# Four accumulator banks in the first expert layer, branch hints one body ahead, and a written order on three engines

## The chip, the core and the metric

The kernel runs on one core of a Trainium2 chip. The metric is the device time of one execution in microseconds (us). The core has a matrix engine (PE, with a separate weight-load side, PEld), a vector engine (DVE), a scalar engine (ACT), a general engine (POOL) and a sync engine (SP). Each has its own instruction stream and waits for the others by semaphores. An engine's sequencer also runs branches and register loads; those are not counted as busy time. Code is brought to the engines by DMA, in its own two queues ("instruction" in the profile's table of queues), beside the data.

## What is computed

Two stages run one after the other. The first is a recurrent attention over 4 batches, 8 heads, 768 steps and a head width of 64; the kernel does it in chunks of 128 steps. The second is a mixture of 8 experts, each a two-layer network, with one expert per token and no token dropped:

```python
logits = x @ w_gate                      # x: 3072 tokens x 512
expert_idx = np.argmax(logits, axis=1)
gate_w = probs[np.arange(N), expert_idx]
for e in range(E):                       # 8 experts
    h = np.maximum(x_sorted[lo:hi] @ w1[e], 0.0)   # 512 -> 1024
    y_sorted[lo:hi] = h @ w2[e]                    # 1024 -> 512
return gate_w[:, None] * y
```

How many tokens an expert has is known only at run time.

## The kernel before

**Attention and routing.** A loop over 24 steps (6 chunks of 4 batches) does the attention. After each chunk, `logits` and `place` find each token's expert and its place in that expert's list. The logits of a chunk stand in the one accumulator bank of the tag "lg" (line 299), and DVE reads them there at lines 319 and 320. The last chunk's routing is woven on PE with the first 256 tokens of expert 0 ("early": `xTa`, `hTa`, `oa`). Then `cnt` (lines 433 and 434), also in the bank "lg", counts the tokens of every expert. DVE turns the counts into `arm`, eight small integers (lines 437 to 445).

**The eight jobs.** One job per expert (loop at line 469). A job has a body for each possible width, from 128 to 512 columns (tokens) in steps of 32: 13 bodies, 5 for expert 0. `tc.Switch` (line 479) makes ACT and PE branch to the body that `arm` asks for; in the last job POOL branches too. A body is: the first layer, eight fills of one accumulator bank each (`layer1`, f = 0 to 7: four accumulating products, which the profile counts as 8 MATMUL), each emptied by ACT with Relu into `hT`; then `turn`, 16 transposes of the next job's tokens, copied out by ACT; then the second layer, one tile of 128 tokens at a time (`layer2`), copied out by ACT into `o`. Each body begins with a hint that names its own exit (printed as line 479) and ends with a branch to the code behind all bodies (printed as the last lines, 590). There the next job's branch stands. So each boundary between jobs has two branches per engine: out of the old body, and into the new one.

**Accumulator banks.** There are eight: "tr" has 3, "sc" 2, "y" 2 and "lg" 1. `layer1` takes the two of "sc" in turn, so PE can fill f = 0 and 1 and must then wait until ACT has emptied f = 0.

**Order.** Inside the bodies PE and ACT follow the written order (line 478). Around them a scheduler places the work: it put all eight loads of `arm` into registers ahead of the first branch, and it spread POOL's indirect gathers (`xs` from `x_d`) and scatters (`o` to the output) over the jobs, so that a job's last two scatters run a job later. SP brings `w1t` and `w2t` (2 MB each) for the job after next as soon as a buffer comes free. Behind the eight jobs a branch skips code for experts with more than 512 tokens, which these inputs don't need.

Of the kernel before, what the change touches and what calls it, by code (L numbers as in the profile page):

```python
# [12 lines left out]
F32 = mybir.dt.float32  # L13
# [7 lines left out]
P = 128  # L21
# [29 lines left out]
def kernel(  # L51
# [11 lines left out]
    nc = tc.nc  # L63
    B, H, S, D = q.shape
    N, DM = out.shape
    E = w_gate.shape[1]
# [4 lines left out]
    DT = DM // P  # L71
    FT = F // P
    W = 512
    TC = W // P
    EARLY = 256
# [9 lines left out]
    def ps(tag, bufs, name):  # L85
        return psum.tile([P, 512], F32, tag=tag, name=name, bufs=bufs)
# [25 lines left out]
    def rt(shape, name, dt=F32):  # L112
        return route.tile(shape, dt, tag=name, name=name)
# [23 lines left out]
    def weights(pool, e):  # L137
        w1t = pool.tile([P, 1, DT, F], F32, tag="w1t", name="w1t")
        w2t = pool.tile([P, 1, FT, DM], F32, tag="w2t", name="w2t")
        nc.sync.dma_start(w1t, w1v[:, ds(e, 1), :, :])  # L140
        nc.sync.dma_start(w2t, w2v[:, ds(e, 1), :, :])
        return w1t, w2t

    first = ctx.enter_context(tc.tile_pool(name="first", bufs=1))
    xs2 = [first.tile([P, TC, DM], F32, tag=f"xs{i}", name=f"xs{i}") for i in range(2)]
# [3 lines left out]
    def gather(xs, idx, tiles, rows=N):  # L149
        for t in tiles:  # L150
            nc.gpsimd.indirect_dma_start(  # L151
                out=xs[:, t, :], out_offset=None, in_=x_d[0:rows, :],
                in_offset=bass.IndirectOffsetOnAxis(ap=idx[:, t : t + 1], axis=0), bounds_check=rows - 1,
                oob_is_err=False)
# [22 lines left out]
    def turn(xs, xT, tiles, evict):  # L177
        for t in tiles:
            tr = ps("tr", 3, "trs").rearrange("p (a t) -> p a t", a=DT)
            for dt in range(DT):  # L180
                nc.tensor.transpose(tr[:, dt, :], xs[:, t, ts(dt, P)], ident)
            evict(out=xT[:, :, ts(t, P)], in_=tr)

    def layer1(n, xT, w1t, hT, f):
        hp = ps("sc", 2, "hp")[:, 0:n]
        for dt in range(DT):
            nc.tensor.matmul(hp, lhsT=w1t[:, 0, dt, ts(f, P)], rhs=xT[:, dt, 0:n], start=(dt == 0),  # L187
                             stop=(dt == DT - 1))
        nc.scalar.activation(out=hT[:, f, 0:n], in_=hp, func=AF.Relu)  # L189

    def layer2(n, hT, w2t, o, t):

        m = min(n - t * P, P)
        parts = P // m if m in (P // 4, P // 2) else 1
        y = ps("y", 2, "ye")
        c = DM // parts
        for f in range(FT):
            for j in range(parts):
                nc.tensor.matmul(y[j * m : j * m + m, 0:c], lhsT=hT[:, f, t * P : t * P + m],  # L199
                                 rhs=w2t[:, 0, f, ts(j, c)], start=(f == 0), stop=(f == FT - 1))  # L200
        for j in range(parts):
            nc.scalar.copy(out=o[0:m, t, ts(j, c)], in_=y[j * m : j * m + m, 0:c])  # L202

    def scatter(o, idx, tiles):
        for t in tiles:
            done = nc.gpsimd.indirect_dma_start(  # L206
                out=out[:, :], out_offset=bass.IndirectOffsetOnAxis(ap=idx[:, t : t + 1], axis=0), in_=o[:, t, :],
                in_offset=None, bounds_check=N - 1, oob_is_err=False)

            tc.declare_no_dep(done.ins, group="scatters", reason="other rows of the output")  # L210
            tc.add_to_no_dep_group("scatters", done.ins)


    with ExitStack() as actx:
# [191 lines left out]
        for n in range(len(steps)):  # L406
# [6 lines left out]
            last, done = done, retain(n)  # L413
# [6 lines left out]
        with tc.manual_schedule(engines={mybir.EngineType.PE}):  # L420
            turn(xs2[0], xTa, range(EARLY // P), nc.vector.tensor_copy)
            for f in range(FT):
                layer1(EARLY, xTa, wa[0], hTa, f)
                if f != 4:
                    next(rest, None)
            for _ in rest:
                pass
            for t in range(EARLY // P):
                layer2(EARLY, hTa, wa[1], oa, t)
# [6 lines left out]
    arm = rt([P, E], "arm", I32)  # L436
    nc.vector.tensor_copy(ne, cnt)

    STEP, LEAST, MOST = 32, P // 32, W // 32
# [8 lines left out]
    PE, ACT, POOL = mybir.EngineType.PE, mybir.EngineType.Activation, mybir.EngineType.Pool  # L448


    mp = ctx.enter_context(tc.tile_pool(name="mp", bufs=2))
    keep2 = ctx.enter_context(tc.tile_pool(name="keep2", bufs=1))
    o2 = [keep2.tile([P, TC, DM], F32, tag=f"o{i}", name=f"o{i}") for i in range(2)]
    for t in o2:
        nc.vector.memset(t, 0.0)
    sets = [wa, weights(keep2, 1)]
    cols = [(src_i[:, ts(e, TC)], dst_i[:, ts(e, TC)]) for e in range(E)]
    HALF = EARLY // P

    gather(xs2[1], cols[0][0], range(HALF, TC))  # L460
    gather(xs2[0], cols[1][0], range(TC))
    xT = mp.tile([P, DT, W], F32, tag="xTs", name="xTs")
    turn(xs2[1], xT, range(HALF, TC), nc.vector.tensor_copy)

    def regs(e, engines):
        return {g: nc.engines[g].value_load(arm[0:1, e : e + 1], min_val=0,
                                            max_val=MOST - LEAST - (EARLY // STEP if e == 0 else 0)) for g in engines}

    for e in range(E):
        w1t, w2t = sets[e]  # L470
        skip = EARLY if e == 0 else 0
        arms = MOST - LEAST + 1 - skip // STEP
        engines = [PE, ACT] + ([POOL] if e == E - 1 else [])
        which = regs(e, engines)
        if e + 1 < E:
            xTn = mp.tile([P, DT, W], F32, tag="xTs", name="xTs")
        hT = mp.tile([P, FT, W], F32, tag="hT", name="hT", bufs=1)
        with tc.manual_schedule(engines={PE, ACT}):
            for a in tc.Switch(which, arms):
                n = STEP * (LEAST + a)  # L480
                for f in range(FT):
                    layer1(n, xT[:, :, skip:], w1t, hT, f)
                if e + 1 < E:
                    turn(xs2[e % 2], xTn, range(TC), nc.scalar.copy)
                tiles = -(-n // P)
                for t in [tiles - 1] + list(range(tiles - 1)):
                    layer2(n, hT, w2t, o2[e % 2], t)
                    if e == E - 1:
                        scatter(o2[e % 2], cols[e][1], [t])
        if e + 1 < E:  # L490
            tiles = range(TC - HALF) if e == 0 else range(TC)
            scatter(o2[e % 2], cols[e][1][:, HALF:] if e == 0 else cols[e][1], tiles)
            xT = xTn
        if e + 2 < E:
            gather(xs2[(e + 1) % 2], cols[e + 2][0], range(TC))
            sets.append(weights(first if e % 2 == 0 else keep2, e + 2))


    most = rt([P, 1], "most")
    over = rt([P, 1], "over", I32)  # L500
    nc.vector.tensor_reduce(most, ne, axis=AX.X, op=ALU.max)
    nc.vector.tensor_scalar(out=over, in0=most, scalar1=float(W), scalar2=None, op0=ALU.is_gt)
    more = nc.values_load(over[0:1, 0:1], min_val=0, max_val=1)
    with tc.If(more > 0), tc.tile_pool(name="op", bufs=1) as op:

# [51 lines left out]
        for j in range(OV):  # L557
            ev = nc.sync.value_load(whose[0:1, j : j + 1], min_val=0, max_val=E - 1)
            w1t, w2t = weights(keep2, ev)
            gather(xs2[j % 2], osrc_i[:, ts(j, TC)], range(TC))  # L560
            xT = mp.tile([P, DT, W], F32, tag="xTs", name="xTs")
            hT = mp.tile([P, FT, W], F32, tag="hT", name="hT", bufs=1)
            turn(xs2[j % 2], xT, range(TC), nc.vector.tensor_copy)
            for f in range(FT):
                layer1(W, xT, w1t, hT, f)
            for t in range(TC):
                layer2(W, hT, w2t, o2[j % 2], t)
            scatter(o2[j % 2], odst_i[:, ts(j, TC)], range(TC))
# [25 lines left out]
```

## Time and profile before

| | |
|---|---|
| time, median of 3 runs | 649.59 us (635.12 to 657.23) |
| profiled execution, its own time | 627.53 us |
| its span, first to last instruction | 625.7 us |
| PE busy | 563.8 us (90%) |
| ACT busy | 123.8 us (20%) |
| POOL busy | 118.8 us (19%) |
| DVE busy | 108.5 us (17%) |
| granted TensorE clock, mean | 0.947 |

The span falls into two parts: attention and routing up to about 227 us, then the eight jobs. Start times of the jobs' first layers on PE are 227.47, 245.54, 298.64, 352.27, 409.37, 457.84, 512.39 and 563.62 us; their widths in this run are 128, 416, 416, 448, 352, 416, 384 and 416 columns. In a row of a timeline the bracket gives the idle time just before the group, and what ended it; "issue" there means that the engine waited for nothing the profile shows, as it does while its sequencer stands at a branch.

### The profile page before, as it was taken

The page shows a single profiled execution, that of the slowest core. Times are in us where ns is not written, and L with a number is a line of the kernel's source. Part 1 is how long each engine was busy: PE and PEld are TensorE (multiplying, and loading weights), DVE is VectorE, ACT ScalarE, POOL GpSimd, SP SyncE. Part 2 cuts the span into 40 slices and gives each one's busy share as a digit, 9 for nine tenths or more (in the row PEclk, how much of TensorE's full clock was granted, in tenths as well). Part 3 has the DMA queues.
Part 4 walks back from the last instruction along what each step waited for, and adds up shares of the span by engine and source line. Part 5 has one row for each costly group of instructions (what it writes and reads, how often), then busy time and mean ns, then how long its engine had stood idle before and what let it go on. Part 6 is the DMA issues. An engine that isn't in the chain of part 4 may idle for free.

```text
span 625.7 us, 7784 instructions
## 1 busy us (share of the span) xinstructions
PE 563.8 (90%) x3160; PEld 371.6 (59%) x3160; DVE 108.5 (17%) x291; ACT 123.8 (20%) x245; POOL 118.8 (19%) x156
## 2 busy tenths in 40 slices
PE   4999999999999988799799989969979996999990
PEld 4988989898988664364355445436435543545540
DVE  2445555466453220000000000000000000000000
ACT  2223232323232211130012012002001201201100
POOL 8331312222220433002102200210310010000011
PEclk9997979899999999899899979999998997999996
DMA  9964647956120449513504410450550314000011
GB/s 186 211 126 124 137 129 213 316 124 159 34 89 14 132 125 381 192 47 137 186 0 170 134 75 18 170 187 0 190 183 0 139 43 147 0 4 20 4 37 50
DMA packets 96476, 72.50 MB, mean 116 GB/s; under 512 B 77946, under 2 KB 77946, under 8 KB 96384
## 3 DMA queue, kind: packets, MB, share of 16 engines
q1 hardware_dynamic: 88096, 52.46, 31.4%
q0 software_dynamic: 5120, 12.60, 5.9%
q10 hardware_dynamic: 3168, 6.29, 2.7%
q8 instruction: 48, 0.79, 0.6%
q14 instruction: 44, 0.36, 0.2%
HBM read 60.84 MB, written 14.68 MB: 121 GB/s over the span
## 4 chain that ended last, share of the span: by engine, by line
issue 56%; PE 28%; POOL 8%; DVE 4%; DMA 1%; POOLq 1%; SPq 0%; DVEq 0%
PE y L288 7%; POOL out_dram L206 4%; PE sc L260 4%; POOL xs L151 4%; PE tr L246 4%; PE y L284 4%; PE lg L308 3%; PE new L269 2%; PE hp L187 2%; PE trx L303 2%; DVE am L262 1%; DMA q<-in_q_dram 1%; DVE xT L305 0%; DVE state L276 0%; SPq L232 0%
## 5 line engine op out<-in xcount | busy, mean ns | idle before, releaser
L187 PE MATMUL hp<-xTs,w1t 128*128 128x416 f32 (+4 forms) x512 | 177.9, 509 | 31.5 <-ACT hT L189 27.8
L187 PEld LDWEIGHTS hp<-xTs,w1t 128*128 128x128 f32 x512 | 98.4, 204 | 111.4 <-issue 66.5
L199 PE MATMUL ye<-w2t,hT 128*128 128x512 f32 (+3 forms) x640 | 164.0, 455 | 0.0
L199 PEld LDWEIGHTS ye<-w2t,hT 128*128 128x128 f32 (+3 forms) x640 | 74.8, 155 | 84.2 <-issue 83.2
L206 POOL DMA_INDIRECT out_dram<-o,dst x30 | 29.8, 995 | 294.3 <-ACT o L202 236.7
L189 ACT ACTIVATE hT<-hp 128x416 f32<-128x416 f32 (+4 forms) x64 | 30.0, 480 | 178.5 <-PE hp L187 123.7
L288 PE MATMUL y<-vs,am 128*128 128x64 f32 x384 | 59.8, 276 | 1.6 <-DVE am L262 0.9
L288 PEld LDWEIGHTS y<-vs,am 128*128 128x128 f32 x384 | 54.5, 202 | 4.5 <-issue 1.8
L202 ACT COPY o<-ye 128x512 f32<-128x512 f32 (+3 forms) x40 | 17.7, 444 | 144.6 <-PE ye L199 144.3
L151 POOL DMA_INDIRECT xs<-x_d,src x30 | 30.3, 1009 | 72.6 <-PE ye L199 35.5
L262 DVE TENSOR_TENSOR am<-sc,causal 128x512 f32<-128x512 f32 x48 | 31.3, 685 | 41.7 <-PE sc L260 41.7
L284 PE MATMUL y<-stb,qT 128*128 128x128 f32 x160 | 37.6, 319 | 0.0
L260 PE MATMUL sc<-qT,kT 64*128 64x128 f32 x384 | 36.3, 300 | 0.9 <-DVE am L262 0.9
L279 POOL COPY stb<-state 64x256 f32<-64x256 f32 x40 | 19.6, 490 | 80.0 <-DVE state L276 78.9
L241 POOL TENSOR_TENSOR vs<-v,dec 128x512 f32<-128x512 f32 x24 | 25.4, 1062 | 38.5 <-PE new L269 25.7
L260 PEld LDWEIGHTS sc<-qT,kT 64*128 64x128 f32 x384 | 28.9, 196 | 5.2 <-issue 4.2
L291 ACT COPY xg<-y 128x512 f32<-128x512 f32 x24 | 14.1, 589 | 84.4 <-PE y L288 84.4
L284 PEld LDWEIGHTS y<-stb,qT 128*128 128x128 f32 x160 | 25.6, 202 | 1.3
L246 PE MATMUL tr<-ident,qs 128*128 128x128 f32 x96 | 18.5, 318 | 7.0 <-DVE qs L240 7.0
L308 PE MATMUL lg<-wg,xT 128*128 128x8 f32 x192 | 24.5, 254 | 0.3
L308 PEld LDWEIGHTS lg<-wg,xT 128*128 128x128 f32 x192 | 23.4, 192 | 1.7 <-DVE xT L305 1.2
L248 ACT COPY qT<-tr 128x512 f32<-128x512 f32 x24 | 14.1, 587 | 37.6 <-PE tr L246 37.6
(111 smaller groups left out, 340.4 us busy)
## 6 DMA issues: line engine op xcount, KB each, us to landing
w1t<-in_moe_w_dram SPq DMA_DIRECT2D x8, 2048.0 KB, 8.0
w2t<-in_moe_w_dram SPq DMA_DIRECT2D x8, 2048.0 KB, 12.0
q<-in_q_dram SPq DMA_DIRECT2D x24, 256.0 KB, 4.6
k<-in_k_dram SPq DMA_DIRECT2D x24, 256.0 KB, 3.2
v<-in_v_dram SPq DMA_DIRECT2D x24, 256.0 KB, 4.4
x_d<-xg ACTq DMA_DIRECT2D x6, 1024.0 KB, 4.4
xs<-x_d,src POOLq DMA_INDIRECT x30, 3.5
out_dram<-o,dst POOLq DMA_INDIRECT x30, 7.1
```

The costliest lines, as they stand in the source:

```text
L151: nc.gpsimd.indirect_dma_start(out=xs[:, t, :], out_offset=None, in_=x_d[0:rows, :], in_offset=bass.IndirectOffsetOnAxis(ap=idx[:, t : t + ...
L187: nc.tensor.matmul(hp, lhsT=w1t[:, 0, dt, ts(f, P)], rhs=xT[:, dt, 0:n], start=(dt == 0), stop=(dt == DT - 1))
L189: nc.scalar.activation(out=hT[:, f, 0:n], in_=hp, func=AF.Relu)
L199: nc.tensor.matmul(y[j * m : j * m + m, 0:c], lhsT=hT[:, f, t * P : t * P + m], rhs=w2t[:, 0, f, ts(j, c)], start=(f == 0), stop=(f == FT ...
L206: done = nc.gpsimd.indirect_dma_start(out=out[:, :], out_offset=bass.IndirectOffsetOnAxis(ap=idx[:, t : t + 1], axis=0), in_=o[:, t, :], i ...
L241: nc.gpsimd.tensor_tensor(out=vs, in0=vt, in1=inner(gk, D), op=ALU.mult)
L246: nc.tensor.transpose(tr[:, a, :], src[:, 2 * a : 2 * a + 2, :].rearrange("p h d -> p (h d)"), ident)
L260: nc.tensor.matmul(sc[j][:, a, :], lhsT=kT[r, a, :], rhs=qT[r, a, :], start=True, stop=True)
L262: nc.vector.tensor_tensor(out=am[j], in0=sc[j], in1=middle(causal[:, :], HP), op=ALU.mult)
L284: nc.tensor.matmul(y[:, ts(a, P)], lhsT=qT[:, a, :], rhs=stb[b][c % 2][:, a, :], start=True, stop=False, skip_group_check=True)
L288: nc.tensor.matmul(y[:, ts(h, D)], lhsT=am[j][:, a, :], rhs=vs[:, h, :], start=(c == 0), stop=True, skip_group_check=True)
L308: nc.tensor.matmul(lg[:, b, :], lhsT=xT[:, dt, :], rhs=wg[:, dt, :], start=(dt == 0), stop=(dt == DT - 1))
```

## The change

`layer1` takes its accumulator from four places by f modulo 4: twice "sc", then "lg", then "tr". The register load of `arm` for job e + 1 stands ahead of job e's branch instead of all loads standing ahead of the first. In each body, ahead of its last tile of the second layer, a hint names the body that the next job will branch to. The code from the first gathers to the end of the jobs follows the written order on PE, ACT and now POOL. The computation of `most` and `over` stands earlier in the text.

```diff
+    hp_tags = [("sc", 2), ("sc", 2), ("lg", 1), ("tr", 3)]
     def layer1(n, xT, w1t, hT, f):
-        hp = ps("sc", 2, "hp")[:, 0:n]
+        hp = ps(*hp_tags[f % len(hp_tags)], "hp")[:, 0:n]
...
+    def regs(e):
+        engines = [PE, ACT] + ([POOL] if e == E - 1 else [])
+        return {g: nc.engines[g].value_load(arm[0:1, e : e + 1], ...) for g in engines}
+
+    with tc.manual_schedule(engines={PE, ACT, POOL}):
+        gather(xs2[1], cols[0][0], range(HALF, TC))
+        gather(xs2[0], cols[1][0], range(TC))
+        which = regs(0)
+        tc.switch_hint(which, arms_of(0), label="job0")
+        xT = mp.tile([P, DT, W], F32, tag="xTs", name="xTs")
+        turn(xs2[1], xT, range(HALF, TC), nc.vector.tensor_copy)
+        for e in range(E):
...
+            if not last:
+                nxt = regs(e + 1)
...
-        with tc.manual_schedule(engines={PE, ACT}):
-            for a in tc.Switch(which, arms):
+            for a in tc.Switch(which, arms_of(e), hint=f"job{e}"):
...
                 for t in [tiles - 1] + list(range(tiles - 1)):
+                    if not last and t == max(tiles - 2, 0):
+                        tc.switch_hint({g: nxt[g] for g in (PE, ACT)}, arms_of(e + 1), label=f"job{e + 1}")
                     layer2(n, hT, w2t, o2[e % 2], t)
```

PE, from the last product of the routing to the first job, before (`hp<-xTa` and `ye<-w2t,hTa` are the early tokens' two layers, `trs` the transposes ahead of the first job):

```order
L434 LDWEIGHTS ones_b
L434 MATMUL cnt<-acc,ones_b 128x8
L187 MATMUL hp<-xTa,w1t 128x256 x8
L199 MATMUL ye<-w2t,hTa 128x512 x16
L181 MATMUL trs<-ident,xs_104 128x128 x8
L466 TENSOR_LOAD arm
L466 ISA x2
```

And PE in the changed kernel at the same place (its lines are two further down):

```order
L189 MATMUL hp<-xTa,w1t 128x256 x8
L201 MATMUL ye<-w2t,hTa 128x512 x16
L436 LDWEIGHTS ones_b
L436 MATMUL cnt<-acc,ones_b 128x8
L471 TENSOR_LOAD arm
L471 ISA x2
L478 SWITCH_STRIDE
L478 ISA
L478 BRANCH_PREFETCH_HINT
L181 MATMUL trs<-ident,xs_104 128x128 x8
```

The count moved from ahead of the last fill to behind the whole early second layer, and the first load of `arm`, which waits for the count, now stands ahead of the transposes.

ACT in the widest body of job 1 and behind it, in the changed kernel:

```order
L191 ACTIVATE hT<-hp 128x512 x8
L182 COPY xTs<-trs 128x4x128 x4
L204 COPY o_2401<-ye 128x512 x3
L498 SWITCH_STRIDE
L498 ISA
L498 BRANCH_PREFETCH_HINT
L204 COPY o_2401<-ye 128x512
L597 UNCONDITIONAL_BRANCH
L471 TENSOR_LOAD arm
L471 ISA x2
L597 SWITCH_STRIDE
L597 ISA x2
```

Before, the four copies stood together, and the exit was followed at once by the next branch (`SWITCH_STRIDE`, `ISA x2`). New are the hint ahead of the last copy and the load of `arm` between the two branches.

POOL around the boundaries behind jobs 1 and 2, before:

```order
L206 DMA out_dram<-o_2401,dst 3072x512
L151 DMA xs_104<-x_d,src 128x512 x4
L206 DMA out_dram<-o_2401,dst 3072x512
L590 UNCONDITIONAL_BRANCH
L206 DMA out_dram<-o_2401,dst 3072x512 x2
L206 DMA out_dram<-o_2400,dst 3072x512
L151 DMA xs_103<-x_d,src 128x512 x4
L206 DMA out_dram<-o_2400,dst 3072x512
```

And in the changed kernel:

```order
L208 DMA out_dram<-o_2401,dst 3072x512 x4
L151 DMA xs_103<-x_d,src 128x512 x4
L597 UNCONDITIONAL_BRANCH
L208 DMA out_dram<-o_2400,dst 3072x512 x4
L151 DMA xs_104<-x_d,src 128x512 x4
```

All four scatters of a job now stand ahead of the four gathers, and none is left for the job after.

## Rows read from the trace of the kernel before

**Rows 1.** Who waited for whom: us in total, times, longest.

```profile
PE hp L187 <- ACT hT L189: 27.8, 7, 5.3
ACT hT L189 <- issue: 54.8, 6, 11.0
```

**Rows 2.** Timeline of PE, jobs 1, 2 and 7: start us, us.

```profile
245.54 5.83 PE L187 MATMUL hp<-xTs,w1t 128*128 128x416 f32 x16 [2.05 <-issue]
255.75 18.60 PE L187 MATMUL hp<-xTs,w1t 128*128 128x416 f32 x48 [4.39 <-ACT hT L189]
...
298.64 5.75 PE L187 MATMUL hp<-xTs,w1t 128*128 128x416 f32 x16
...
570.11 17.03 PE L187 MATMUL hp<-xTs,w1t 128*128 128x416 f32 x48 [0.74 <-ACT hT L189]
```

**Rows 3.** Fills 2 to 7 of jobs 1 to 7: length, PE busy, clock.

```profile
468.22:488.10 19.88, 19.88 (x48) 10.31 (x48) 0.85 0.00 1
...
570.11:587.14 17.03, 17.03 (x48) 9.04 (x48) 1.00 0.00 0
sum 131.09, PE 131.07 PEld 69.96; mean PE 18.72 PEld 9.99
```

**Rows 4.** Timeline of ACT, boundaries ahead of jobs 2 and 4.

```profile
298.84 0.59 ACT L202 COPY o<-ye 128x512 f32<-128x512 f32 x1 [6.28 <-PE ye L199]
307.84 0.93 ACT L189 ACTIVATE hT<-hp 128x416 f32<-128x416 f32 x2 [8.41 <-issue]
...
419.09 0.82 ACT L189 ACTIVATE hT<-hp 128x352 f32<-128x352 f32 x2 [8.93 <-issue]
```

**Rows 5.** ACT's sequencer, 298 to 309 us: durations ns, first and last start.

```profile
L590 ACTq COMPARE_BRANCH  x2: 38/42/47, 298.9 to 301.4; - x2
L590 ACTq MOVE  x2: 29/29/29, 301.2 to 301.3; - x2
...
L479 ACTq BRANCH_PREFETCH_HINT  x1: 31/31/31, 307.7 to 307.7; - x1
```

**Rows 6.** PE's sequencer: its branches, 285 to 300 us, then the whole run.

```profile
L590 PEldq COMPARE_BRANCH  x2: 313/2362/4412, 290.9 to 291.6; - x2
...
L590 PEldq COMPARE_BRANCH  x16: 300/403/8082, 226.5 to 602.0; - x16
```

**Rows 7.** The loads of `arm` into registers, ACT and PE: ns min/median/max.

```profile
L466 ACTq TENSOR_LOAD <-arm x8: 272/277/472, 209.2 to 213.5; - x8
...
L466 PEldq TENSOR_LOAD <-arm x8: 299/308/493, 220.4 to 225.5; - x8
```

**Rows 8.** Timeline of PE around the count and the first job.

```profile
207.40 0.17 PE L434 MATMUL cnt<-acc,ones_b 128*128 128x8 bf16 x1
...
224.70 1.04 PE L181 MATMUL trs<-ident,xs 128*128 128x128 f32 x8
227.47 7.38 PE L187 MATMUL hp<-xTs,w1t 128*128 128x128 f32 x64 [1.73 <-DVE xTs L182]
```

**Rows 9.** Timeline of DVE: the last read of "lg", the count, `arm`.

```profile
200.49 0.19 DVE L320 TENSOR_TENSOR dl<-lg,mx 128x32 f32<-128x32 f32 x1
...
207.74 0.16 DVE L437 COPY ne<-cnt 128x8 f32<-128x8 f32 x1
...
209.04 0.14 DVE L445 TENSOR_SCALAR arm<-arm 128x1 int32<-128x1 int32 x1
```

**Rows 10.** Timeline of POOL: the last three scatters.

```profile
610.72 0.98 POOL L206 DMA_INDIRECT out_dram<-o,dst  x1 [5.88 <-ACT o L202]
614.01 0.98 POOL L206 DMA_INDIRECT out_dram<-o,dst  x1 [2.31 <-issue]
615.30 0.98 POOL L206 DMA_INDIRECT out_dram<-o,dst  x1 [0.30 <-issue]
```

**Rows 11.** DMA issues of the page: KB each, us to landing.

```profile
w2t<-in_moe_w_dram SPq DMA_DIRECT2D x8, 2048.0 KB, 12.0
...
xs<-x_d,src POOLq DMA_INDIRECT x30, 3.5
```

More of the change, by code (lines that the diff above doesn't have):

```diff
@@ L458 @@
     HALF = EARLY // P
[L460 to L477, printed above, removed]
-        with tc.manual_schedule(engines={PE, ACT}):
-            for a in tc.Switch(which, arms):
[L480 to L496, printed above, removed]
     most = rt([P, 1], "most")
@@ L502, with arms_of @@
     nc.vector.tensor_scalar(out=over, in0=most, scalar1=float(W), scalar2=None, op0=ALU.is_gt)
+    def arms_of(e):
+        return MOST - LEAST + 1 - (EARLY // STEP if e == 0 else 0)
+    def regs(e):
+        engines = [PE, ACT] + ([POOL] if e == E - 1 else [])
+        return {g: nc.engines[g].value_load(arm[0:1, e : e + 1], min_val=0, max_val=arms_of(e) - 1) for g in engines}
+    with tc.manual_schedule(engines={PE, ACT, POOL}):
[6 more added lines that the diff above has]
+        for e in range(E):
+            w1t, w2t = sets[e]
+            skip = EARLY if e == 0 else 0
+            last = e == E - 1
+            if not last:
+                nxt = regs(e + 1)
+                xTn = mp.tile([P, DT, W], F32, tag="xTs", name="xTs")
+            hT = mp.tile([P, FT, W], F32, tag="hT", name="hT", bufs=1)
+            for a in tc.Switch(which, arms_of(e), hint=f"job{e}"):
+                n = STEP * (LEAST + a)
+                for f in range(FT):
+                    layer1(n, xT[:, :, skip:], w1t, hT, f)
+                if not last:
+                    turn(xs2[e % 2], xTn, range(TC), nc.scalar.copy)
+                tiles = -(-n // P)
+                for t in [tiles - 1] + list(range(tiles - 1)):
+                    if not last and t == max(tiles - 2, 0):
+                        tc.switch_hint({g: nxt[g] for g in (PE, ACT)}, arms_of(e + 1), label=f"job{e + 1}")
+                    layer2(n, hT, w2t, o2[e % 2], t)
+                    if last:
+                        scatter(o2[e % 2], cols[e][1], [t])
+            if not last:
+                scatter(o2[e % 2], cols[e][1][:, HALF:] if e == 0 else cols[e][1], range(TC - HALF if e == 0 else TC))
+                xT, which = xTn, nxt
+            if e + 2 < E:
+                gather(xs2[(e + 1) % 2], cols[e + 2][0], range(TC))
+                sets.append(weights(first if e % 2 == 0 else keep2, e + 2))
     more = nc.values_load(over[0:1, 0:1], min_val=0, max_val=1)
```

## The prediction

> **What bounds the kernel now.** I read the table of busy times first: PE is busy for nine tenths of the span, so the other tenth, and what makes busy PE slow, is all a change of order can win. The view of waits names it: seven times PE's first layer waits for ACT's `hT`, 27.8 us together, and ACT itself stands still for "issue" just ahead of its `hT`, 54.8 us in six times [rows 1]. The timeline of PE places this. Job 1 fills two banks in 5.83 us, waits 4.39 us, and needs 18.60 us for the six fills that are left; job 7 waits 0.74 us and needs 17.03 us for six fills of the same width [rows 2]. So a wait costs twice. [...]
>
> The timeline of ACT shows why it is late. Its last copy of job 1 ends at 299.43 us, its first Relu of job 2 starts at 307.84, 8.41 us later, while PE began job 2 at 298.64 [rows 2, 4]. ACT's sequencer has two branches in the gap: from the exit branch at 298.9 to the next instruction at 301.2 pass 2.3 us, from the entry branch at 301.4 to the new body's first instruction at 307.7 pass 6.3 us [rows 5]. PE's own branches there cost 0.31 us (exit) and 4.41 us (entry), but its sequencer comes to them at 290.9, 7.7 us before PE is through with the old job [rows 2, 6], and nothing is seen of them. So at each boundary PE stands still because ACT's code comes late, with two banks to bridge the time.
>
> **The change, part by part.**
>
> *Four banks.* PE can start four fills before it needs the first bank again. Six fills of 416 columns take 17.03 us at full clock [rows 2], so one takes 2.84 us and four 11.35 us. In job 2 ACT has emptied the first bank at 307.84 + 0.47 = 308.31, 9.67 us after PE began [rows 2, 4]. Even if no hint helps and ACT's new register load adds 0.6 us (0.28 us for the load [rows 7], the rest for the two register instructions behind it), that is 10.3 us, within 11.35. So the wait goes: −27.8 us (between −22 and −27.8). Nothing new is late in its place at these widths: ACT then catches up, a Relu of 0.47 us against a fill of 2.84 us.
>
> *The clock behind the wait.* The six fills of jobs 1 to 7 took 131.09 us in all [rows 3]. At job 7's rate (17.03 us per 416 columns) their 4 × 416 + 448 + 352 + 384 = 2848 columns are worth 116.6 us. Without the waits the difference goes: −14.5 us (between −9 and −14.5, if some short idle still lowers the clock).
>
> *Hint for the next body.* On ACT it is executed ahead of the last tile's copy, some 6.9 us before the old body ends (the copy at 298.84 waited 6.28 us and the one before it took about 0.6 [rows 4]). That is as long as the loaded entry branch of 6.3 us, so most of that branch should go; ACT would then be some 3.5 us late instead of 9.7. With four banks this is worth nothing at 416 columns. On PE it lies under the 7.7 us lead, except into job 1, where the old body is short and PE stood 2.05 us for issue [rows 2]: −1.0 us (0 to −2.05), the middle, since there the hint comes only just ahead of the branch.
>
> *Register loads at each boundary.* 0.3 us each on PE [rows 7], about 0.7 us with the register work: under the lead of 7.7 us on PE and under the four fills on ACT. Nothing; without that cover seven times 0.7, 5 us.
>
> *POOL's written order.* Tail: the last scatter starts at 615.30 now, because two of job 6's follow job 7's last one at 610.72 [rows 10]. These two go forward by a job, −4.6 us; but POOL's 2.31 us without work between, at its own exit branch, comes back to the path in part: −3.5 us (−2 to −4.6). Gathers: they now stand behind four scatters. Scatter to scatter is 1.29 us [rows 10], so four scatters and four gathers are issued in about 10.4 us, from about 1.1 us after PE began the next job. A gather lands 3.5 us after issue, and the 2 MB of `w2t` that start at that moment land in 12.0 us [rows 11]: the last gather lands 15 us after the job's start, 19 if it shares the way. The transposes that need it come after eight fills, 8 × 2.84 = 22.7 us, or 19.2 us at 352 columns. Nothing, with 0 to 4 us of slack in the narrowest job.
>
> *The count, later.* This one costs. Now the count is read long before `arm` is needed; the early second layer hides everything. In the changed order PE counts where it began the transposes (224.70 [rows 8]). The copy came 0.34 us after the count, and the last step on `arm` ended 1.44 us after the copy began [rows 8, 9]. Then a load of 0.5 us [rows 7] and about 0.8 us of register work and hint, with the count's own 0.2 us: the transposes start 3.3 us later. The third early fill takes "lg", which DVE reads until 200.68 [rows 9], so PE waits there for about 0.6 us. Together +3.9 us (2 to 6). PE then idles some 3 us ahead of the transposes. Idle of 0.74 us left the clock at 1.00, idle of 4 to 5 us cost 14.5 / 6 = 2.4 us each [rows 2, 3]; I take half, +1.2 us (0 to 3).
>
> Sum: −27.8 − 14.5 − 1.0 − 3.5 + 3.9 + 1.2 = −41.7 us against the profiled execution's 627.53, so 586 us. All favourable ends give 581, all unfavourable ones 604.
>
> **How that stands to the median.** The runs' median is 649.59, 22 us above the profiled execution, and the fastest run was 635.12. No row tells where the 22 us lie. If they lie in work that stays, the new time is 649.6 − 41.7 = 608; if they lie in longer waits for code and the low clock behind them, which go, it is 586. I take the middle, **598 us**.
>
> **Rivals.**
>
> *The hints do nothing* (the change does not do all it says). For it: the old bodies already begin with a hint for their exit, and ACT still spent 2.3 us there [rows 5]. Against it: PE's exit, hinted alike, cost 0.31 us [rows 6]. Then the four banks work alone. At 352 columns four fills take 9.6 us, and ACT's first bank is free about 0.8 + 8.93 + 0.41 + 0.6 = 10.7 us after PE's start (0.8 as in rows 4 from PE's start to the end of the copy): 1.1 us; with as much again in jobs 1 and 6, 3 us in all. Time 601. [...]
>
> *ACT later than four banks.* The hint for the next body might take the place of the exit's, so that the exit, too, is paid under load. At 6.3 us each, both branches, 0.6 us of register load and 0.8 + 0.5 us around them free the first bank 14.5 us after PE's start, 3.2 us beyond the four fills. Times six, with 2.4 us of low clock each, that gives back 33 us of the 42: 631 on the median's scale. For it: in the old kernel a body gives a single hint, so no row shows how two in one body get on. Against it: exits come before `w2t` loads the queues.
>
> *TensorE's own branches, slower than before.* If the exit hint on PE is lost to the new one and the new one fails, PE pays two unprepared branches. It decides from 7.7 + 4 = 11.7 us for the two (the lead and the wait of today), since then PE stands longer than now. The dearest branch of PE cost 8.08 us [rows 6]; two of these and 0.7 us make 16.9, so 9.2 us of idle at seven boundaries: 64 us in place of 27.8, the clock's loss stays, and with +5.1 and −3.5 for the ends the time is 649.6 + 38 = 688. Against it: 8.08 is the maximum of 16, the exits lie near 0.3.
>
> **How the numbers follow.** The forecast has 0.55, hints without effect 0.30, ACT beyond four banks 0.08, PE's own branches 0.03; 0.04 is left for what I do not see, such as a gather that comes late. Range 580 to 622: from the favourable end without any of the open 22 us (581) to near the unfavourable end with nearly all of them (604 + 18); the first rival lies inside. A measurement of this kernel can tell about 2% from no change, here 637 to 663. Faster by over 2%: 0.55 + 0.30, and most of the rest but for PE's branches, 0.90; within 2% 0.07; slower 0.03.
>
> **What would show it.** Right: in the changed profile the wait of PE's `hp` for ACT's `hT` is under 4 us; six fills of 416 columns take about 17.0 us in every job, and the clock is 1.00 there; ACT's gap at a boundary falls from 8.4 to 3 or 4 us; the first job's first fill starts near 231 us; the last scatter starts within 1 us of ACT's last copy. Wrong: ACT's gap stays at 9 us (first rival), grows beyond 12 us with a wait at the fifth fill (second), PE's first fill of a job stands behind several us of "issue" (third), or PE waits for a gather's DMA ahead of the transposes.

## The result and the profile after

The changed kernel takes **591.75 us**, the median of 4 runs (583.62 to 601.95), beside 642.36 us for the kernel before on the same chip: a ratio of **0.931 (95% interval 0.912 to 0.951)**. Five more rounds on another chip gave 598.86 us beside 641.18, ratio 0.929 (0.917 to 0.940). The ratios leave disturbed runs out, so they are not exactly the quotients of these medians. The forecast was 598, with a range of 580 to 622.

The profiled execution took 591.75 us, its span 589.9 (625.7 before), at a mean granted clock of 0.954 (0.947 before). Where the time went, by starts of groups on the timelines of PE and ACT:

| stretch | before, us | after, us | difference |
|---|---|---|---|
| span's start to PE's first early fill (attention, routing) | 195.3 | 200.9 | +5.6 |
| first early fill to job 0's first fill | 32.2 | 37.0 | +4.8 |
| job 0's first fill to job 1's | 18.07 | 17.92 | −0.2 |
| job 1's first fill to the end of ACT's last copy | 364.9 | 321.0 | −43.9 |
| ACT's last copy to the end (tail) | 15.3 | 13.2 | −2.1 |

From the first early fill on, that is 430.5 us before and 389.1 after, −41.4. The change does not touch the stretch ahead of it: PE's products, and the instructions of DVE, ACT and SP, are the same there in both traces.

The seven jobs from job 1 on fell from 53.1, 53.6, 57.1, 48.5, 54.5, 51.2 and 46.8 us to 46.8, 46.8, 50.2, 41.6, 46.8, 43.0 and 45.8. PE now goes through them without a pause, as its groups of instructions between 255 and 569 us show (busy us, mean ns of one, then idle time before them):

```profile
L189 PE MATMUL hp<-xTs,w1t 128*128 128x416 f32 (+3 forms) x448 | 154.4, 505 | 0.0
L201 PE MATMUL ye<-w2t,hT 128*128 128x512 f32 (+3 forms) x611 | 151.6, 449 | 0.0
```

The wait of 27.8 us [rows 1] is gone, and nothing stands in its place. The timeline of PE (start us, us; the bracket is the idle time ahead):

```profile
200.87 3.66 PE L189 MATMUL hp<-xTa,w1t 128*128 128x256 f32 x8 [0.78 <-DVE xTa L182]
...
208.09 3.69 PE L189 MATMUL hp<-xTa,w1t 128*128 128x256 f32 x16 [0.60 <-DVE dl L322]
...
232.67 0.17 PE L436 MATMUL cnt<-acc,ones_b 128*128 128x8 bf16 x1
235.64 1.96 PE L181 MATMUL trs<-ident,xs 128*128 128x128 f32 x8 [2.81 <-issue]
237.83 9.28 PE L189 MATMUL hp<-xTs,w1t 128*128 128x128 f32 x64 [0.23 <-DVE xTs L182]
...
302.55 22.51 PE L189 MATMUL hp<-xTs,w1t 128*128 128x416 f32 x64
...
399.57 19.36 PE L189 MATMUL hp<-xTs,w1t 128*128 128x352 f32 x64
```

In job 2 all 64 products stand in one group now, where [rows 2] had 16, a wait, and 48. Ahead of the jobs the new idle of 2.81 us is to be seen, and behind it job 0's fills take 9.28 us in place of 7.38 [rows 8]. The first early fill, too, is slower than before, though it stands ahead of all that the change moves: 3.66 us at a granted clock of 0.54, where the kernel before has 1.99 us at 1.00:

```profile
195.27 1.99 PE L187 MATMUL hp<-xTa,w1t 128*128 128x256 f32 x8 [0.78 <-DVE xTa L182]
```

The clock of the jobs' first layers, by the table of stretches (length, PE busy, PEld busy, clock, DMA share, GB/s; seven stretches, first layers of jobs 1 to 7):

```profile
302.55:325.06 22.51, 22.51 (x64) 11.97 (x63) 1.00 0.50 168
...
399.57:418.93 19.36, 19.36 (x64) 11.89 (x63) 1.00 0.59 197
...
sum 154.42, PE 154.41 PEld 83.70; mean PE 22.06 PEld 11.96
```

All seven have 1.00. In [rows 3] job 5 had 0.85.

ACT is still late. Its timeline at the boundaries ahead of jobs 2 and 4, and its sequencer ahead of job 2 (durations ns, first and last start):

```profile
302.75 0.59 ACT L204 COPY o<-ye 128x512 f32<-128x512 f32 x1 [6.28 <-PE ye L201]
311.00 1.33 ACT L191 ACTIVATE hT<-hp 128x416 f32<-128x416 f32 x3 [7.66 <-issue]
...
408.68 1.53 ACT L191 ACTIVATE hT<-hp 128x352 f32<-128x352 f32 x4 [8.32 <-issue]
```

```profile
L597 ACTq COMPARE_BRANCH  x2: 37/55/73, 302.8 to 306.1; - x2
...
L489 ACTq BRANCH_PREFETCH_HINT  x1: 36/36/36, 310.9 to 310.9; - x1
```

The gap was 8.41 and 8.93 us [rows 4] and is 7.66 and 8.32. The entry branch at 306.1 leads to the new body's first instruction at 310.9, 4.8 us, where [rows 5] has 6.3. The exit with the load of `arm` takes from 302.8 to 306.1. So ACT empties its first bank about 9 us after PE began the job. PE has four banks to fill meanwhile, 11.3 us at 416 columns (22.51 / 8 = 2.81 each) and 9.7 at 352.

POOL's last scatter, by its timeline, and its place behind ACT's last copy:

```profile
577.03 0.98 POOL L208 DMA_INDIRECT out_dram<-o,dst  x1 [5.89 <-ACT o L204]
```

Nothing follows it; in [rows 10] two scatters of the job before came 4.58 us behind this one.

### The profile page after: what moved, and what is told of

The parts are those of the page before. It is cut to its first block, busy times and chain, and to the rows that moved or that the text cites. A ratio compares the mean times of both kernels' runs of the same rounds, so it can differ in the third digit from the quotient of the medians.

```text
span 589.9 us, 7874 instructions
## 1 busy us (share of the span) xinstructions
PE 558.0 (95%) x3160; PEld 374.7 (64%) x3160; DVE 109.6 (19%) x291; ACT 123.3 (21%) x245; POOL 119.0 (20%) x156
## 4 chain that ended last, share of the span: by engine, by line
PE 54%; issue 34%; DVE 4%; POOL 3%; DMA 2%; SPq 0%; POOLq 0%; DVEq 0%
PE hp L189 13%; PE ye L201 11%; PE y L290 7%; PE sc L262 5%; PE tr L248 4%; PE y L286 4%; PE lg L310 4%; PE new L271 2%; PE trx L305 2%; POOL xs L151 2%; DMA out_dram<-o,dst 1%; PE trs L181 1%; POOL out_dram L208 1%; DVE am L264 1%; DMA q<-in_q_dram 1%
## 5 line engine op out<-in xcount | busy, mean ns | idle before, releaser
L189 PE MATMUL hp<-xTs,w1t 128*128 128x416 f32 (+4 forms) x512 | 163.7, 482 | 0.2 <-DVE xTs L182 0.2
L189 PEld LDWEIGHTS hp<-xTs,w1t 128*128 128x128 f32 x512 | 94.2, 195 | 70.1 <-issue 54.9
```

## Experiments

**Theory.** The four banks bring nearly all: they bridge ACT's late code, and with the wait goes the low clock behind it. The late count gives some 5 us back. **Rival 1:** the hints, not the banks, bring ACT in time. **Rival 2:** the loads ahead of each job and POOL's order bring much of it. "Jobs 1 to 7" below is the stretch from job 1's first fill to the end of ACT's last copy, 364.9 us before and 321.0 after; expectations quote it 0.6 us shorter, up to the start of that copy.

**1. Four banks alone, in the kernel before.**

```diff
+    hp_tags = [("sc", 2), ("sc", 2), ("lg", 1), ("tr", 3)]
-        hp = ps("sc", 2, "hp")[:, 0:n]
+        hp = ps(*hp_tags[f % len(hp_tags)], "hp")[:, 0:n]
```

> The kernel before with nothing but the four accumulator places. Theory (the banks bring the gain): PE's wait for ACT's hT falls from 27.8 us to 0 to 3 us, ACT's gap at a boundary stays at 8 to 9 us, and the stretch from job 1's first fill to ACT's last copy (364.3 us before, 320.4 us in the changed kernel) is 320 to 326 us. Rival (the hints bring a good part, by making ACT earlier): the wait stays above 8 us and the stretch above 335 us. The count moves behind the early second layer here too, so 3 to 5 us between that layer and job 0 are lost in both cases.

Measured: 607.47 us (4 runs), before 645.71, ratio 0.950 (0.915 to 0.985). PE's wait for `hT` is 0.4 us and jobs 1 to 7 take 323.2: the banks alone win 41.7 of the 43.9 us. ACT's entry stayed at 5.7 to 6.9 us ahead of jobs 1 to 6. The tail stayed at 15.3. What it costs lies ahead of job 0, on PE's timeline and its sequencer:

```profile
237.41 0.17 PE L436 MATMUL cnt<-acc,ones_b 128*128 128x8 bf16 x1
237.44 1.07 PE L181 MATMUL trs<-ident,xs 128*128 128x128 f32 x8
247.17 8.71 PE L189 MATMUL hp<-xTs,w1t 128*128 128x128 f32 x64 [8.66 <-issue]
...
266.81 24.28 PE L189 MATMUL hp<-xTs,w1t 128*128 128x416 f32 x64 [2.29 <-DMA xs<-x_d,src]
```

```profile
L468 PEldq TENSOR_LOAD <-arm x8: 295/305/503, 240.0 to 245.2; - x8
```

The count is late here too, with nothing but the table of banks changed: so the banks move it. The scheduler still puts all eight loads ahead of the first branch, 240.0 to 245.2, and with the count late nothing covers them: 8.66 us of idle where the changed kernel has 2.81. From the end of the early second layer to job 0's first fill pass 9.59 us, in the changed kernel 5.00. So the change's loads one job ahead are worth some 4.6 us by this comparison (they were not run alone), but only because its banks made the count late. I had 3 to 5 us for the whole loss against before, and it is 9.59 − 2.60 = 7.0. Ahead of job 1 PE also waits 2.29 us for a gather, and the fills behind take 24.28 us, 22.51 in the changed kernel: that is most of the 2.2 us that jobs 1 to 7 take more here.

**2. Two banks, all else of the change.**

```diff
-    hp_tags = [("sc", 2), ("sc", 2), ("lg", 1), ("tr", 3)]
+    hp_tags = [("sc", 2)]
```

> The changed kernel with the old two places for the fills; hints, loads and order as changed. Theory (the banks): ACT's gap is still 7.5 to 9 us, so PE waits 22 to 28 us for hT, at 0.84 to 0.91 of the clock behind it, and the stretch from job 1's first fill to ACT's last copy is 355 to 366 us. Rival (the hints): ACT's gap is 3 to 4 us, the wait under 8 us, the stretch under 335 us.

Measured: 628.4 us (6 runs), ratio 0.976 (0.952 to 0.999); jobs 1 to 7 take 360.7, only 4.2 less than before. The count is early again, 1.75 us from the early layer's end to job 0's first fill. The waits, and PE in jobs 2 and 3:

```profile
PE hp L189 <- ACT hT L191: 25.3, 6, 5.7
...
ACT hT L191 <- issue: 55.6, 7, 10.1
```

```profile
313.35 5.75 PE L189 MATMUL hp<-xTs,w1t 128*128 128x416 f32 x16
322.86 19.98 PE L189 MATMUL hp<-xTs,w1t 128*128 128x416 f32 x48 [3.76 <-ACT hT L191]
...
376.21 20.00 PE L189 MATMUL hp<-xTs,w1t 128*128 128x448 f32 x48 [2.91 <-ACT hT L191]
```

With every hint in place the old wait and the slow fills behind it (19.98 us for 17.03; in job 3, at 448 columns, 20.00 for 17.03 × 448 / 416 = 18.3) are back. Rival 1 falls.

**3. Four banks, no hint one body ahead.**

```diff
-        tc.switch_hint(which, arms_of(0), label="job0")
-            for a in tc.Switch(which, arms_of(e), hint=f"job{e}"):
+            for a in tc.Switch(which, arms_of(e)):
-                    if not last and t == max(tiles - 2, 0):
-                        tc.switch_hint({g: nxt[g] for g in (PE, ACT)}, ...)
```

> The changed kernel without the hints for the next body (each body's hint for its own exit stays). Theory (hints without effect on the end): stretch from job 1's first fill to ACT's last copy 319 to 323 us, no wait for hT over 2 us in all; ACT's entry branch 4 to 6.5 us as with hints; PE's entry branch back from 2.0 to about 4.4 us and its two slow exits (3.6 and 3.9 us) back to 0.3 to 0.4, all under PE's lead. Rival: ACT's entry branch goes above 6.5 us and PE waits more than 5 us for hT in all.

Measured: 599.14 us (4 runs), ratio 0.943 (0.910 to 0.976); jobs 1 to 7 take 323.6, 2.6 more than with hints. PE in job 4 (352 columns), and ACT's branches there:

```profile
396.92 9.63 PE L189 MATMUL hp<-xTs,w1t 128*128 128x352 f32 x32
407.98 9.73 PE L189 MATMUL hp<-xTs,w1t 128*128 128x352 f32 x32 [1.43 <-ACT hT L191]
```

```profile
L594 ACTq COMPARE_BRANCH  x2: 43/45/47, 397.1 to 400.5; - x2
...
L488 ACTq BRANCH_PREFETCH_HINT  x1: 35/35/35, 407.3 to 407.3; - x1
```

Now the entry takes 6.8 us (400.5 to 407.3), and in the narrowest job four banks are just too few: the fifth fill waits 1.43 us. So the hints do something: ahead of jobs 1 to 6 ACT's entry is 5.7 to 6.9 us without them and 4.1 to 5.3 with them. But the worth is 2.6 us of 43.9, at the narrow jobs (the only other wait is 0.78 us in job 6), and, ahead of this stretch, 1.72 us for issue that PE stands into job 1 again. Wait and entry lie just beyond what I had expected (2.2 us in all for at most 2, 6.8 for at most 6.5), the wait far from the rival's 5 us. The prediction's rival "the hints do nothing" had put 1.1 us of wait there and 3 us in all.

**4. The changed kernel with two banks for the early tokens only.**

```diff
-    def layer1(n, xT, w1t, hT, f):
-        hp = ps(*hp_tags[f % len(hp_tags)], "hp")[:, 0:n]
+    def layer1(n, xT, w1t, hT, f, tags=hp_tags):
+        hp = ps(*tags[f % len(tags)], "hp")[:, 0:n]
-                layer1(EARLY, xTa, wa[0], hTa, f)
+                layer1(EARLY, xTa, wa[0], hTa, f, [("sc", 2)])
```

> The changed kernel with the early fills on the two old places, so that the count of tokens again stands ahead of the last early fill; the jobs keep four places. Theory (the late count costs 3 us of idle PE, and the low clock behind it): from the end of the early second layer to job 0's first fill 2.5 to 3.0 us instead of 5.2, job 0's fills 7.4 us instead of 9.3, no wait of PE for the last read of the logits bank; 4 to 6 us less than the changed kernel in the stretch from the early first fill to job 1. Rival (the time is bound there by the gather or by code, not by the count): the first fill stays at 5 us behind the early second layer.

Measured: 596.45 us (4 runs). The profile is clearer than that time: from the first early fill to the end 381.3 us, where the changed kernel has 389.1. PE's timeline:

```profile
220.74 1.99 PE L189 MATMUL hp<-xTa,w1t 128*128 128x256 f32 x8 [0.78 <-DVE xTa L182]
...
232.86 0.17 PE L436 MATMUL cnt<-acc,ones_b 128*128 128x8 bf16 x1
...
250.16 1.04 PE L181 MATMUL trs<-ident,xs 128*128 128x128 f32 x8
251.85 7.38 PE L189 MATMUL hp<-xTs,w1t 128*128 128x128 f32 x64 [0.65 <-PE trs L181]
```

The count stands 17 us ahead of the transposes again, the 2.81 us of idle are gone, the transposes take 1.04 us in place of 1.96, and job 0's fills 7.38 in place of 9.28. From the early layer's end to job 0's first fill pass 1.52 us, less than the 2.5 to 3.0 expected. Of the 7.7 us between the two profiles, 1.7 are not the count's: the first early fill, ahead of it, took 1.99 us here and 3.66 in the changed kernel. It took 1.99 us, too, in three variants with the late count (experiments 3, 5 and 7). So the late count cost about 6 us, at the upper end of the 4 to 6 expected.

**5. Three banks.**

```diff
-    hp_tags = [("sc", 2), ("sc", 2), ("lg", 1), ("tr", 3)]
+    hp_tags = [("sc", 2), ("sc", 2), ("lg", 1)]
```

> The changed kernel with three accumulator places for the fills instead of four. Theory (PE waits as long as ACT's lateness exceeds the banks): ACT frees the first bank 8.8 to 9.7 us after PE's start (from the changed kernel's trace), three fills take 8.4 us at 416 columns, 7.1 at 352 and 7.7 at 384, so PE waits 0.4 to 1.3 us per boundary at 416 columns and 1.5 to 2.5 at 352 and 384, 6 to 9 us in all; idle this short leaves the clock at 1.00, so the stretch from job 1's first fill to ACT's last copy is 327 to 331 us. Rival (any wait brings the low clock back): the same waits, but 0.85 to 0.9 of the clock behind them and a stretch of 337 us or more.

Measured: 595.15 us (one run); jobs 1 to 7 take 329.1, 8.1 more than with four. PE in jobs 2 and 4:

```profile
298.19 8.54 PE L189 MATMUL hp<-xTs,w1t 128*128 128x416 f32 x24
307.87 14.23 PE L189 MATMUL hp<-xTs,w1t 128*128 128x416 f32 x40 [1.14 <-ACT hT L191]
...
397.12 7.26 PE L189 MATMUL hp<-xTs,w1t 128*128 128x352 f32 x24
407.51 12.10 PE L189 MATMUL hp<-xTs,w1t 128*128 128x352 f32 x40 [3.12 <-issue]
```

Three banks bridge 8.5 us at 416 columns, and ACT's 9 us leave a wait of 1.14; at 352 columns it is 3.12. In all 6.7 us of waits. The fills behind them run at full rate (14.23 / 5 = 2.85 us each, and 12.10 / 5 = 2.42 at 352 columns, where the changed kernel has 19.36 / 8 = 2.42 at a clock of 1.00): idle of up to 3.1 us cost no clock here. In experiment 2 the fills behind 3.76 us of idle were slower, but so were those behind 2.91 us there (20.00 us for 18.3) and behind 2.29 us in experiment 1 (24.28 for 22.51), so the length of the idle alone did not decide it. The fourth bank is needed, by about 1 us in the wide jobs.

**6. The hint earlier in the body.**

```diff
-                    if not last and t == max(tiles - 2, 0):
+                    if not last and t == tiles - 1:
```

> The changed kernel with the hint for the next body ahead of the first tile of the second layer instead of the last, about 14 us sooner. [...] Theory 2 (the hint came too late to finish): the entry branch falls below 1 us and ACT's gap from 7.7 to 8.6 us to about 4. [...]

Measured: 599.19 us (one run); jobs 1 to 7 take 322.2. ACT ahead of job 2:

```profile
L597 ACTq COMPARE_BRANCH  x2: 37/55/73, 309.4 to 313.8; - x2
...
L489 ACTq BRANCH_PREFETCH_HINT  x1: 36/36/36, 318.5 to 318.5; - x1
```

The entry takes 4.7 us, 4.6 to 5.5 ahead of jobs 1 to 6, with ACT's hint some 16 us sooner (22.2 us ahead of PE's start of job 2, 6.4 in the changed kernel). More time ahead did not make the hint on ACT work better (4.7 us for 4.8 ahead of job 2), so the lead was not what limited it.

**7. POOL left to the scheduler.**

```diff
-    with tc.manual_schedule(engines={PE, ACT, POOL}):
+    with tc.manual_schedule(engines={PE, ACT}):
```

> The changed kernel with the written order on PE and ACT alone; the scheduler places POOL's gathers and scatters, which puts the gathers a job sooner and leaves two scatters of job 6 for the end, as in the kernel before. Theory (POOL's order is worth the tail alone): from ACT's last copy to the end 15.3 us instead of 13.2, everything from job 1 to ACT's last copy as in the changed kernel, 320 to 322 us. Rival (the gathers' new place costs time): that stretch gets shorter by over 2 us, or w2t lands in 12 us instead of 15 and ACT's entry branches get shorter.

Measured: 595.11 us (one run); jobs 1 to 7 take 320.9, the tail 15.3. POOL's last three scatters:

```profile
578.29 0.98 POOL L208 DMA_INDIRECT out_dram<-o,dst  x1 [5.88 <-ACT o L204]
581.56 0.98 POOL L208 DMA_INDIRECT out_dram<-o,dst  x1 [2.28 <-issue]
582.85 0.98 POOL L208 DMA_INDIRECT out_dram<-o,dst  x1 [0.30 <-issue]
```

It is the old tail of [rows 10]. POOL's written order is worth 2.1 us at the end and nothing in jobs 1 to 7. `w2t` landed in 11.4 us (15.0 in the changed kernel), as the rival had it, but ACT's entries stayed at 4.2 to 5.3; the kernel of experiments 4 and 8 has 12.0 and 16.1 us in its two profiles. Ahead of job 1 PE stood 0.81 us here that it does not in the changed kernel; its cause was not followed. With experiment 1, rival 2 falls: from these two parts come 2.1 us, and some 4.6 that only make good part of what the banks cost.

**8 and 9. The kernel of experiment 4 and the changed kernel, five rounds side by side.** The edit of 8 is that of experiment 4; 9 is the changed kernel as it stands.

> The version with the count ahead of the last early fill once more, timed in five rounds beside the changed kernel. Theory: from the early first fill to the end of the span it takes 381 to 383 us (the changed kernel 389), so its times lie 5 to 8 us below the changed kernel's, about 583 to 588 us in the middle; the spread of both, some 20 us, lies ahead of the early first fill, in the attention stage. Rival: what it saves there comes back in the jobs or the tail, and the times are the same.

> The changed kernel itself, five rounds on the same chip. Both theories: 584 to 602 us, 389 us from the early first fill to the end of the span give or take 2 us, and the difference from run to run in the attention stage.

Measured: 585.73 us (7 runs), ratio 0.910 (0.900 to 0.920), and 598.86 us (6 runs), ratio 0.929 (0.917 to 0.940). From the first early fill to the end the profiles have 381.3 and 388.8 us, within 0.3 of the earlier profiles of the same two kernels. So the version with two banks for the early tokens is the best: 7.4 us by the profiles, 13 by the medians. Of the 7.4, 1.7 are again the first early fill's (1.99 and 3.66 us), ahead of what the edit moves. The two intervals overlap by 0.003, so of the 13 us only the nearly 6 that the profiles place behind the edit are shown.

## Why the prediction was right, and where its parts were not

**Four banks, −27.8: right.** The wait is gone (0.0 us in the stretch above). **The clock behind the wait, −14.5: right.** All first layers of jobs 1 to 7 run at 1.00. The two terms gave −42.3, and jobs 1 to 7 fell by 43.9. Experiments 1 and 2 show that the banks do it: banks alone 323.2, all but banks 360.7.

**The hint on ACT: the step that failed.** It said that most of the entry branch should go, since the hint comes as long ahead as the branch takes, and that ACT would be 3.5 us late. The entry fell by about 1.5 us (experiment 3, mean over jobs 1 to 6), the load of `arm` and its register work put some 0.7 back, and ACT's gap ahead of job 2 is 7.66 us, nearer to the first rival's sign (9 us) than to the forecast's (3 or 4). The error cost the forecast nothing, because the term stood at nothing at 416 columns: the four banks bridge the unprepared branch as well, but for 1.43 us in the narrowest job and 0.78 in job 6 (experiment 3).

Experiment 6 excludes too short a lead, and the tables of DMA queues show what was missing. Queue q14 is taken for the one that brings ACT's code, since an 8 KB piece comes on it 0.9 to 1.2 us behind each of ACT's exits. Between ACT's hint for job 2 and its exit (296.19 to 302.75 us) nothing moves on it; the first piece comes after the exit (303 to 310.9 us). In experiment 6 nothing moves there in 22 us (287.05 to 309.4). Queue, pieces, MB and share, in these three windows:

```profile
q8 instruction: 1, 0.02, 0.9%
...
q14 instruction: 2, 0.02, 0.7%
```

```profile
q8 instruction: 4, 0.07, 1.4%
```

It is so at all seven boundaries of both profiles. On PE's side, from job 2 on, one 16 KB piece on q8 follows each hint before the exit. So ACT's hint for the next body brought no code ahead of the exit; behind the entry one piece fewer comes than in the kernel before (one for two up to job 5, two for three in jobs 6 and 7), which may be what saved the 1.5 us. Why no piece follows ACT's hint is open, and so is how much of the entry is the load on the DMA engines: ahead of job 2 their busy share is 0.96 during the entry's 4.73 us, ahead of job 7 it is 0.57 during 1.98 us, by the table of stretches (306.13 to 310.86 and 533.87 to 535.85 us). No run changes that load alone. In each of ACT's entries ahead of jobs 1 to 7, in the kernel before and in the changed one, one to three pieces of 8 KB come on q14 between the branch and the new body; in PE's exits of 0.3 to 0.4 us, hinted alike, none comes on q8.

**The hint on PE.** Job 1 now starts without the 2.05 us for issue of [rows 2], with which I had counted for half. Elsewhere it is off the path, as said. PE's sequencer, at the boundaries ahead of jobs 2 and 5, then over the whole run, and over the whole runs of experiments 3 (no such hints) and 6 (hints sooner):

```profile
L597 PEldq COMPARE_BRANCH  x2: 440/1212/1984, 294.8 to 296.3; - x2
...
L597 PEldq COMPARE_BRANCH  x2: 1991/2798/3605, 433.4 to 438.1; - x2
...
L597 PEldq COMPARE_BRANCH  x16: 293/1988/4562, 236.8 to 568.3; - x16
```

```profile
L594 PEldq COMPARE_BRANCH  x16: 303/405/7106, 232.0 to 568.1; - x16
```

```profile
L597 PEldq COMPARE_BRANCH  x16: 307/2796/4925, 243.3 to 576.0; - x16
```

The entry ahead of job 2 took 1.98 us, 4.41 before [rows 6]. Ahead of job 5 the exit took 3.61 us, where exits cost 0.3 to 0.4; the one into job 7 took 3.9. The second rival feared this for ACT; it came on PE, at two of the seven boundaries behind jobs 0 to 6. The new hint causes it: without it (experiment 3) all seven exits take 0.3 to 0.4 us, with it sooner (experiment 6) six of seven take 3.5 to 3.8, and a 16 KB piece of code comes in each slow exit and in no cheap one. That the hint takes the place of the exit's own fits this, but no run shows it. PE's sequencer was through at 440.1 us, 1.0 us before job 5's first fill at 441.13: nothing was lost, but not by much.

**POOL's order: −3.5 predicted, −2.1 measured** (experiment 7 gives it alone), near the unfavourable end of −2. The last scatter moved ahead by the 4.6 us that were said, but from its start to the end now pass 12.9 us, 10.4 before, so POOL's 2.31 us came back whole. Gathers: right, PE waits for none of them in the stretch above.

**The count, later: +3.9 predicted, 3.6 measured,** in the two waits of PE that the prediction named, 2.81 us ahead of the transposes and 0.60 us for "lg", and the count's own 0.17. The count's copy and the last step on `arm`, on DVE's timeline:

```profile
232.90 0.17 DVE L439 COPY ne<-cnt 128x8 f32<-128x8 f32 x1 [15.85 <-PE cnt L436]
...
233.97 0.15 DVE L447 TENSOR_SCALAR arm<-arm 128x1 int32<-128x1 int32 x1
```

The last step ends at 234.12, and PE's transposes begin 1.5 us later, after the load and the hint. **The low clock behind it: +1.2 predicted, about 2.8 measured** (transposes 1.96 us for 1.04, at a granted clock of 0.50 for 1.00; fills 9.28 for 7.38, at 0.79 for 1.00), near the end of 3 us. Against them stand 1.5 us that PE no longer waits behind the transposes (0.23 us for 1.73 [rows 8]), which the prediction did not see. By the stretches it is 6.7 us in all (4.8 ahead of job 0, 1.9 in its fills), less the 1.7 of the first early fill, which belong to neither term: 5.0 for 5.1 predicted. Beside the version with two banks for the early tokens it is about 6 (experiments 4, 8 and 9).

So the sum of terms, −41.7, met −41.4 from the first early fill on. In part that is luck of the signs: jobs 1 to 7 gave 1.6 us more than said and the start of job 1 1.1 more, while the first early fill, in no term, took 1.7 more and the tail gave 1.4 less. Job 0's first fill, named for 231 us, came at 237.83; 5.6 us of that are the attention's and 1.7 the first early fill's.

**The open 22 us.** I took the middle between "in work that stays" and "in what goes". The profiles speak for the first. Eleven of them, of this kernel and its variants, were taken; two pairs are of one and the same kernel, and agree within 0.3 us from the first early fill on. Up to that fill they differ by up to 25.6 us, with the same code there: 195.3 us before and 198.0 to 220.9 in the others, 200.9 and 207.3 in the two of the changed kernel. It goes with the clock, though not strictly: by the trace's record of the granted clock, the profile before had 20.5 us at the lower level there (0.50 in it and in the changed kernel's, beside 1.00), those with 220.7 and 220.9 had 47.8, and two with 51.2 had 207.3 and 207.4. One stretch of attention, in the kernel before and then in the changed one (length, PE busy, clock, DMA share, GB/s):

```profile
115.00:133.00 18.00, 17.32 (x183) 0.91 0.92 216
```

```profile
115.00:133.00 18.00, 17.38 (x118) 0.53 0.77 192
```

PE is busy alike, but gets through 118 products in place of 183, at 0.53. The runs that were only timed have no trace, so that their spread is the same thing is likely, not shown. By that reading 649.6 − 41.7 = 608 was the consistent number, and the 591.75 us of the first four runs were a fortunate draw; the larger set, 641.2 before and 598.9 after, differs by 42.3.

## What to carry to other kernels

An engine that comes late at a branch need not be made faster: find what its consumer holds in between, and measure one unit of it (here a bank of 2.81 us) against the lateness (9 us); nearly the whole gain in the jobs came from having enough, and how many banks are enough came out of these two numbers. When a new use of a shared buffer reaches code outside the loop it was meant for, look there for what the scheduler moves: the table of banks, applied to the early tokens, pushed the count behind 17 us of other work and cost about 6 us, which one argument gives back. And where runs spread by more than the terms of the sum, compare the profiles stage by stage before sharing the difference out; here 1.7 us of a slow clock ahead of the change stood in the same stretch as the change's own cost.

## What was not expected of the hardware

- The hints helped differently by engine. From job 2 on PE's entry went from 4.3–4.7 us to 2.0–2.7, and into job 1 from 8.1 to 4.6. On ACT, ahead of jobs 1 to 6, it went from 5.6–6.9 to 4.1–5.3, and no piece of code came for it between hint and exit. ACT's exit, hinted in the old kernel and in the new, takes 2.4 to 3.4 us (5.7 once, ahead of job 1 in the old one), where PE's takes 0.3 to 0.4.
- With a second hint in a body some exits were slow: PE's took over 3 us at none of seven boundaries without it, at two with it, at six with it sooner.
- Idle of 2.81 us ahead of the transposes was followed by the lower clock (0.50 in the transposes, 0.79 in job 0's fills), and idle of 2.29 us in experiment 1 and of 2.91 us in experiment 2 by slower fills (24.28 us for 22.51, 20.00 for 18.3); the fills behind 3.12 us in job 4 of the three-bank kernel kept 2.42 us each. PE had run 13.90 us of products ahead of the first, and a whole job ahead of the last; what made the difference was not tested.
- PE had the lower clock inside attention (0.53 over 115 to 133 us of the changed kernel's profile, 0.91 before) for 20 to 51 us, from one execution to the next, with no change in the code there. Its cause was not tested.
